# A long-convolution gate kernel on one core: the filter response made two pairs ahead, the first spectrum load cut in two, and the inverse result stored block by block

## The chip, the cores and the metric

The kernel runs on one core of one Trainium2 chip. The metric is the device time of one execution in microseconds (us). Three runs of the kernel before took 1207.08, 1214.94 and 1216.21 us (median 1214.94). The trace comes from one further, profiled execution.

The core has five engines with a queue of instructions each: PE (TensorE, matrix products into the PSUM memory), PEld (its weight loads), DVE (VectorE), ACT (ScalarE), POOL (GpSimd) and SP (SyncE, which here only issues DMAs). An engine takes its instructions in order; between engines there are semaphores. DMAs are issued from the queues of SP and ACT.

## The reference

```python
h    = (relu(pos_emb @ w1) @ w2) * exp(-0.01 * pos)      # the filter, S x D
u    = x * v
y    = irfft(rfft(u, 2S) * rfft(h, 2S))[:, :S]           # long convolution along the sequence
x2   = x * y
gate = sigmoid(causal_conv5(x2, conv_w))                 # per channel, 5 taps
out  = (gate * (x2 @ w_val)) @ w_out
```

B = 4, S = 12800, D = 128, 64 filter features, all float32.

## The kernel before

The transform of length 12800 is cut into J = 2 blocks of 6400 = N1 (100) x N2 (64), and both factors are done as matrix products. There are three stages.

**Stage 1** (0 to about 375 us) makes the first transform of u. It has 64 steps n, in 32 pairs q = n // 2 with s = n % 2. A step fetches 800 KB (`fetch`, split by `_Split`, L120, into 96 rows and 4 rows), multiplies x by v on DVE (`product`, L305), and each pair then takes sums and differences: two on DVE (L313) and two differences on POOL (L316). `spectra` (L321) does the matrix products into the PSUM tile `fp` and ACT copies them into `st` (L331, four buffers). `store` (L334) writes `st` to the DRAM tensor `a_u` one step later, as 96 and 4 rows. Between these steps the filter is made by the generator `filt` (L223): its steps are dealt out at a pace that has a number of the n steps as its divisor (L368, here N2 - 2), and its last part (tiles `fk` and `gp`, lines L274 to L288) uses ACT, DVE and PE.

**Stage 2** (about 375 to 804 us) runs over 50 pairs p of frequencies. `load_pair` (L427) brings 1 MB of `a_u` and, for every fourth pair, the tables `w`. `filter_pair` (F, L396) makes the filter's response: PE into a `c_ps` buffer, then three ACT operations into `h_sb` (L407 to L409, three buffers). `spectrum` (S0 and S1, L412) is the second transform: PE into four banks `z_ps`. `times` (L421) multiplies them on DVE: `va` and `vb` use the banks of S0, `vc` and `vd` those of S1. POOL adds (L514 to L516), and `inverse` (I0 and I1, L441) goes back: PE into `c_ps` (two buffers, shared with F), ACT into `c_sb` (L454), and a DMA to the DRAM tensor `c_y` (L457). The order is written out by hand. In one round the engines get: DVE va(p), vb(p), the small sums of p - 1 (L501 to L504), vc(p), vd(p); PE F(p+1), S0(p+1), S1(p+1), I0(p-1), I1(p-1); ACT the copies and DMA issues of I(p-1) and the three operations of F(p+1). DMAs from SP stand in program order.

**Stage 3** (815 us to the end) loads rows of `c_y` into the tile `ag` (`load_k`, L201, for the first three groups; these stand in SP's queue during stage 2 and at its end), sums over N1 on PE (`y_sum`, L597), transposes, multiplies by x and does the gate. `WARM` matrix products (L687), whose result nobody reads, stand on PE between the stages.

Lines used below: L120 the split DMA of stage 1 and 3; L436 the `a_u` loads; L431 the `w` loads; L417 S0 and S1; L402 F on PE; L447 the inverse on PE; L457 the `c_y` stores; L204 the early `ag` loads; L601 the first work of stage 3 on PE.

Of the kernel before, what the change touches and what calls it, by code (L numbers as in the profile page):

```python
# [24 lines left out]
J, N1, N2 = 2, 100, 64  # L25
M = N1 * N2
KG = 8
# [1 line left out]
P0 = NH - NF  # L29
PT = P0 + N1  # L30
R = 4
WARM = 8
NC1 = N1 // 2 + 1


# [88 lines left out]
def tile_longconv_gate(  # L124
# [20 lines left out]
    nc = tc.nc  # L145
# [5 lines left out]
    a_u = dram.tile([N1, 2, N2 // 2, 2, J, B, D], F32, name="a_u")  # L151

    c_y = dram.tile([J, N1, 2 * N2, B, D], F32, name="c_y")
# [30 lines left out]
    def load():  # L184
        return ld.tile([128, 2048], F32, name="ld")
# [10 lines left out]
    FIRST = len(blocks) // 2  # L196
# [4 lines left out]
    def load_k(s, c, k0, k1):  # L201
        j, g = y_order[s]
        n0 = c * N2 + g * R
        nc.sync.dma_start(  # L204
            out=block(s, c)[k0:k1], in_=c_y[j, k0:k1, n0:n0 + R].rearrange("k p b d -> k (p b d)"))


    with tc.tile_pool(name="p1", bufs=1) as p1, tc.tile_pool(name="ps1", bufs=1, space=PSUM) as ps1:
        pos_v = pos.rearrange("(j a n) f -> j a n f", j=J, a=N1)

# [97 lines left out]
        def mirrored(q):  # L308

            a, b = us.pop(2 * q), us.pop(2 * q + 1)  # L310
            eo = held_e[q % 2]
            for s, op in ((0, ALU.add), (1, ALU.subtract)):
                nc.vector.tensor_tensor(  # L313
                    eo[:PT, s].rearrange("p j l e -> p (j l e)"), a[:PT], b[:PT], op=op)
            for s in range(2):
                nc.gpsimd.tensor_tensor(  # L316
                    eo[:PT, s, :, 0], eo[:PT, s, :, 0], eo[:PT, s, :, 1], op=ALU.subtract)
            eos[q] = eo

# [14 lines left out]
        def store(q, s, st):  # L334
            sync_s.dma_start(
                out=a_u[:, s, q].rearrange("k e j b d -> k (e j b d)"),
                in_=st[P0:PT].rearrange("k e j b d -> k (e j b d)"))

        fetched, us, eos, last = {}, {}, {}, None
        with tc.manual_schedule():  # L340
            for t in held:
                nc.gpsimd.memset(t[0:P0], 0.0)
            held_e = [p1.tile([128, 2, J, 2, XE], F32, name=f"eo{i}") for i in range(2)]
            for t in held_e:
                nc.vector.memset(t[96:128], 0.0)
            fetch(0)
            raw_val, raw_out = _raw(nc, p1, w_val, "raw_val"), _raw(nc, p1, w_out, "raw_out")
            raw_cw = _raw(nc, p1, conv_w.rearrange("k d -> d k"), "raw_cw")
            fil = filt()
            n_fil, spent = 16 * 1.3 + 0.7 + 16 * 0.9 + 16 * 1.5 + 25 * 1.9 + 0.5, 0.0  # L350
            for i in range(1, XB):
                fetch(i)
            product(0)
            product(1)
            mirrored(0)
            product(2)
            for i in (XB, XB + 1):
                fetch(i)
            for n in range(N2):
                q, s = divmod(n, 2)  # L360
                if n + XB + 2 < N2:
                    fetch(n + XB + 2)
                if n + 3 < N2:
                    product(n + 3)
                if s == 0 and q + 1 < N2 // 2:
                    mirrored(q + 1)
                st = spectra(q, s)
                while spent < n_fil * (n + 1) / (N2 - 2):  # L368
                    step = next(fil, None)
                    if step is None:  # L370
                        break
                    spent += step
                if last:
                    store(*last)
                last = q, s, st
                if n == 40:
                    _narrow(nc, p1, wval, raw_val)
                if n == 46:
                    _narrow(nc, p1, wout, raw_out)
                if n == 52:  # L380
                    _narrow(nc, p1, cw, raw_cw)
            for _ in fil:
                pass
            store(*last)


    with tc.tile_pool(name="p2", bufs=1) as p2, tc.tile_pool(name="ps2", bufs=1, space=PSUM) as ps2:
        BD = B * D
        NP = N1 // 2
        PG = KG // 2  # L390
        half = [slice(h * N2, (h + 1) * N2) for h in range(2)]

        def bank():
# [18 lines left out]
        def spectrum(p, j):  # L412
            a2, wk = loaded[p]
            zs = bank(), bank()
            for c in range(2):
                for h in range(2):
                    nc.tensor.matmul(  # L417
                        out=zs[c][half[h]], lhsT=wk[half[c], 0, half[h]], rhs=a2[half[c], h, j], start=True, stop=True)
            z_p[p, j] = zs

        def times(out, z, h_sb, n):  # L421

            nc.vector.tensor_tensor(  # L423
                out, z.rearrange("p (b d) -> p b d", d=D).unsqueeze(1).to_broadcast([128, n, B, D]),
                h_sb.unsqueeze(2).to_broadcast([128, n, B, D]), op=ALU.mult)

        def load_pair(p):  # L427
            if p % PG == 0:
                n_p = min(PG, NP - p)
                wt = load().rearrange("p (k c e) -> p k c e", k=PG, c=4)[:, :, 0:3]  # L430
                nc.sync.dma_start(out=wt[:, 0:n_p], in_=t_w[:, p:p + n_p])  # L431
                weights.append(wt)
            a2 = load().rearrange("p (k j e) -> p k j e", k=2, j=J)
            step = 1 if p == 0 else 2
            for i in range(0, 2, step):
                nc.sync.dma_start(  # L436
                    out=a2[:, i:i + step].rearrange("p k j e -> p k (j e)"),
                    in_=a_u[2 * p + i:2 * p + i + step].rearrange("k s n e j b d -> (s n e) k (j b d)"))
            return a2, weights[-1][:, p % PG]

        def inverse(p, j, terms):  # L441
            wk = loaded[p][1]
            c_ps = ps2.tile([128, 2, BD], F32, name="c_ps", bufs=2)
            for i, (c, vt) in enumerate(terms):
                n = vt.shape[1] * D
                for h in range(2):
                    nc.tensor.matmul(  # L447
                        out=c_ps[:, h, 0:n], lhsT=wk[half[h], 1 + c], rhs=vt[half[h]].rearrange("p b d -> p (b d)"),
                        start=(i == 0), stop=(i == len(terms) - 1))
            if j == 0:  # L450
                c_sb = p2.tile([128, 2, J, B, D], F32, name="c_sb", bufs=2)
                outs[p] = c_sb
            c_sb = outs[p]
            nc.scalar.copy(out=c_sb[:, :, j].rearrange("p h b d -> p h (b d)"), in_=c_ps)  # L454
            if j == J - 1:
                for h in range(2):
                    nc.scalar.dma_start(  # L457
                        out=c_y[:, 2 * p + h].rearrange("j p b d -> p j (b d)"),
                        in_=c_sb[:, h].rearrange("p j b d -> p j (b d)"))

        weights, loaded, outs = [], {}, {}
        filt_p, z_p, v_p = {}, {}, {}
        AHEAD = 2
        PB = B // 2
# [1 line left out]
        def start_pair(p):  # L466
            filt_p[p] = filter_pair(p).rearrange("p s j c d -> p s (j c) d")
# [5 lines left out]
        with tc.manual_schedule():  # L473
            for p in range(-1, NP + 1):
                now, nxt, old = 0 <= p < NP, p + 1 < NP, 0 <= p - 1
                for q in range(AHEAD + 1) if p < 0 else (p + AHEAD,):
                    if q < NP and q not in loaded:
                        loaded[q] = load_pair(q)
                if p in early:
                    load_k(*early.pop(p))  # L480
                if p == 41:
                    j, g = y_order[0]
                    nc.sync.dma_start(
                        out=xr_first, in_=xt[j][:, g * R:(g + 1) * R].rearrange("d n b a -> d (n b a)"))
                if p == NP:
                    for s in range(FIRST):
                        for c in range(2):
                            load_k(s, c, 80, 96)
                if now:
                    h = filt_p.pop(p)  # L490
                    z0, z1 = z_p.pop((p, 0)), z_p.pop((p, 1))
                    va = p2.tile([128, 2 * J, B, D], F32, name="va", bufs=3)
                    vb = p2.tile([128, 2 * J, B, D], F32, name="vb", bufs=2)
                    times(va, z0[0], h[:, 0], 2 * J)
                    times(vb, z0[1], h[:, 1], 2 * J)
                if nxt:
                    start_pair(p + 1)
                    spectrum(p + 1, 0)
                if old:
                    oa, oc, od = v_p.pop(p - 1)  # L500
# [21 lines left out]
                    inverse(p - 1, 1, ((0, oa[:, 2]), (1, oa[:, 3, 0:PB]), (0, oc[:, 0]), (1, oc[:, 1])))  # L522
            for s in range(FIRST):
                for c in range(2):
                    load_k(s, c, 96, N1)

    ld_pool.__exit__(None, None, None)

# [6 lines left out]
    with tc.tile_pool(name="p3", bufs=1) as p3, tc.tile_pool(name="ps3", bufs=1, space=PSUM) as ps3:  # L535
# [144 lines left out]
        with tc.manual_schedule():  # L680
# [4 lines left out]
            for _ in range(WARM):  # L685
                w_ps = ps3.tile([D, 2 * D], F32, name="o_ps", bufs=2)
                nc.tensor.matmul(  # L687
                    out=w_ps, lhsT=ident, rhs=dft.rearrange("p a k -> p (a k)"), start=True, stop=True)
            for t in range(-AHEAD3, NT + 2):
                s = t + AHEAD3  # L690
# [79 lines left out]
```

## Time and profile before

| what | value |
|---|---|
| runs | 1207.08, 1214.94, 1216.21 us; median 1214.94 |
| profiled execution | 1216.66 us, its span 1214.6 us |
| mean granted TensorE clock | 0.971 |
| PE busy | 1069.3 us (88% of the span) |
| DVE busy | 979.5 us (81%) |
| POOL busy | 783.6 us (65%) |
| ACT busy | 615.1 us (51%) |
| DMA | 329.92 MB, mean 272 GB/s |

A row of a timeline reads: start in us, duration, engine, line, operation, the tile written and the tile read, shape, count, and in brackets how long the engine had been idle before it and what released it. "SPq" and "ACTq" are DMA issues. A row of windows gives, for a stretch of the span, the busy time of each engine, the granted TensorE clock (1.00 is full), the mean busy share of the sixteen DMA engines, and GB/s.

### The profile page before, as it was taken

Reading aid. Unit: us, or ns where it says so; the run is one execution under the profiler, and the core shown is the slowest. Engines: PE = TensorE matmul, PEld = TensorE weight load, DVE = VectorE, ACT = ScalarE, POOL = GpSimd, SP = SyncE. Lnnn points to the kernel's source line nnn. Section 1 sums busy time; section 2 is a strip of 40 time slices with the busy share of each in tenths; the row PEclk is TensorE's granted clock in tenths of the full one; section 3 lists DMA queues with packets and bytes.
Section 4 is the critical chain, followed back from the end, with each engine's and each line's share of the span. In section 5 each row is a group of like instructions: output and inputs, shape, how many; then the busy total and the mean of one; then the engine's idle time right before and its main releaser. Section 6 shows DMA issues by size and latency. Waiting matters only on the chain. (4 is left out here: it accounts for less than half of the span.)

```text
span 1214.6 us, 17869 instructions
## 1 busy us (share of the span) xinstructions
PE 1069.3 (88%) x6280; PEld 496.0 (41%) x6280; DVE 979.5 (81%) x1166; ACT 615.1 (51%) x1000; POOL 783.6 (65%) x400
## 2 busy tenths in 40 slices
PE   1689888777876999999999999978999999999986
PEld 0445455333442334443443444333444444444432
DVE  4477555588873899999999999926999999999997
ACT  0235654666672234333333433326676776766764
POOL 5134333233322788888888888826898898898880
PEclk9799999999897799999999999989999999999999
DMA  9899999999997578887777998767999989999932
GB/s 218 222 302 335 330 303 311 308 304 306 308 294 279 213 279 287 282 285 278 273 273 270 319 347 287 229 162 215 256 287 283 290 269 278 285 287 279 290 133 108
DMA packets 90976, 329.92 MB, mean 272 GB/s; under 512 B 10102, under 2 KB 17698, under 8 KB 77490
## 3 DMA queue, kind: packets, MB, share of 16 engines
q1 hardware_dynamic: 56912, 249.06, 67.5%
q10 hardware_dynamic: 33978, 79.74, 17.6%
q8 instruction: 51, 0.84, 0.3%
q14 instruction: 35, 0.29, 0.1%
HBM read 197.69 MB, written 131.07 MB: 271 GB/s over the span
## 5 line engine op out<-in xcount | busy, mean ns | idle before, releaser
L628 POOL TENSOR_TENSOR ext<-yr,xr 128x400 f32<-128x400 f32 x120 | 303.2, 2528 | 40.4 <-DVE yr L626 38.2
L316 POOL TENSOR_TENSOR eo<-eo 114x512 f32<-114x512 f32 x64 | 116.3, 1836 | 240.4 <-DVE eo L313 240.4
L329 PE MATMUL fp<-eo,fold 64*128 64x512 f32 x768 | 192.0, 633 | 63.1 <-ACT st L331 45.8
L643 DVE SCALAR_TENSOR_TENSOR gt<-ext,cw,gt 128x1600 f32<-128x1600 f32 x128 | 240.7, 1881 | 0.8 <-ACT gt L640 0.8
L454 ACT COPY c_sb<-c_ps 128x1024 f32<-128x1024 f32 x100 | 101.4, 1014 | 203.6 <-PE c_ps L447 194.2
L331 ACT COPY st<-fp 128x1024 f32<-128x1024 f32 x128 | 124.3, 1015 | 152.4 <-DMA a_u<-st 91.6
L447 PE MATMUL c_ps<-va,ld 64*128 64x512 f32 (+1 forms) x800 | 166.7, 556 | 0.7 <-POOL va L516 0.7
L423 DVE TENSOR_TENSOR va<-z_ps,h_sb 128x2048 f32<-128x2048 f32 x50 | 114.4, 2289 | 54.0 <-ACT h_sb L407 35.1
L417 PE MATMUL z_ps<-ld 64*64 64x512 f32 x800 | 142.3, 624 | 16.3 <-DMA ld<-a_u 7.3
L514 POOL TENSOR_TENSOR va<-va,vb 128x1024 f32<-128x1024 f32 x50 | 118.3, 2365 | 24.1 <-DVE vb L423 24.1
L601 PE MATMUL sd<-ag,inv 100*64 100x512 f32 x512 | 127.2, 612 | 7.3 <-DMA ag<-c_y 6.3
L329 PEld LDWEIGHTS fp<-eo,fold 64*128 64x128 f32 x768 | 73.6, 195 | 141.5 <-issue 81.3
L662 PE MATMUL o_ps<-gd,wout 128*128 128x400 f32 x256 | 112.4, 521 | 19.1 <-DVE gd L657 10.4
L447 PEld LDWEIGHTS c_ps<-va,ld 64*128 64x128 f32 x800 | 74.3, 189 | 114.1 <-issue 111.2
L516 POOL TENSOR_TENSOR va<-va,vb 128x1024 f32<-128x1024 f32 x50 | 118.5, 2370 | 0.0
L608 ACT COPY sd_sb<-sd 128x512 f32<-128x512 f32 x128 | 76.1, 594 | 81.2 <-PE sd L601 61.0
L423 DVE TENSOR_TENSOR vb<-z_ps,h_sb 128x2048 f32<-128x2048 f32 x50 | 114.0, 2280 | 0.0
L652 PE MATMUL v_ps<-ext,wval 128*128 128x400 f32 x256 | 107.1, 500 | 0.0
L447 PE MATMUL c_ps<-vc,ld 64*128 64x512 f32 x400 | 94.2, 589 | 0.0
L515 POOL TENSOR_TENSOR vc<-vc,vd 128x768 f32<-128x768 f32 x50 | 91.1, 1822 | 0.0
L615 PEld LDWEIGHTS tp<-ident,sd_sb 128*128 128x128 f32 x512 | 58.6, 141 | 75.9 <-PE sd L601 49.5
L615 PE MATMUL tp<-ident,sd_sb 128*128 128x128 f32 x512 | 80.3, 281 | 3.1 <-DVE yr L626 2.6
(88 smaller groups left out, 1493.3 us busy)
## 6 DMA issues: line engine op xcount, KB each, us to landing
c_y<-c_sb ACTq DMA_DIRECT2D x100, 512.0 KB
ld<-a_u SPq DMA_DIRECT2D x49, 1024.0 KB
ld<-in_xv_dram SPq DMA_DIRECT2D x64, 768.0 KB
a_u<-st SPq DMA_DIRECT2D x64, 768.0 KB
ag<-c_y SPq DMA_DIRECT2D x116, 384.0 KB
out_dram<-o_sb ACTq DMA_DIRECT2D x32, 800.0 KB
xr<-in_xt_dram SPq DMA_DIRECT2D x31, 800.0 KB
ld<-in_tab_w_dram SPq DMA_DIRECT2D x12, 768.0 KB
```

Source lines behind the costliest of these rows:

```text
L316: nc.gpsimd.tensor_tensor(eo[:PT, s, :, 0], eo[:PT, s, :, 0], eo[:PT, s, :, 1], op=ALU.subtract)
L329: nc.tensor.matmul(out=fp[:, h], lhsT=fold[r, w], rhs=eo[r, o, :, l], start=i == 0, stop=i == len(terms) - 1)
L331: nc.scalar.copy(out=st[:, o].rearrange("k j (h b) d -> k h j (b d)", h=2), in_=fp)
L417: nc.tensor.matmul(out=zs[c][half[h]], lhsT=wk[half[c], 0, half[h]], rhs=a2[half[c], h, j], start=True, stop=True)
L423: nc.vector.tensor_tensor(out, z.rearrange("p (b d) -> p b d", d=D).unsqueeze(1).to_broadcast([128, n, B, D]), h_sb.unsqueeze(2).to_broadc ...
L447: nc.tensor.matmul(out=c_ps[:, h, 0:n], lhsT=wk[half[h], 1 + c], rhs=vt[half[h]].rearrange("p b d -> p (b d)"), start=(i == 0), stop=(i == ...
L514: nc.gpsimd.tensor_tensor(va[:, 0:2], va[:, 0:2], vb[:, 0:2], op=ALU.add)
L516: nc.gpsimd.tensor_tensor(va[:, 2:4], va[:, 2:4], vb[:, 2:4], op=ALU.add)
L601: nc.tensor.matmul(out=sd[c * N2:(c + 1) * N2], lhsT=inv[:, c], rhs=ct[c][:, r * B * D:(r + 1) * B * D], start=True, stop=True)
L615: nc.tensor.transpose(out=tp[:, b], in_=t[:, b], identity=ident)
L628: nc.gpsimd.tensor_tensor(e[:, r0 + r], yr, xr, op=ALU.mult)
L643: nc.vector.scalar_tensor_tensor(gt, rows(t, k), cw[:, k:k + 1], gt, op0=ALU.mult, op1=ALU.add)
```

## The change

The edits, each with where it stands:

1. `WARM` from 8 to 14.
2. The filter's pace in stage 1: divisor N2 - 6 in place of N2 - 2, so that its steps are used up some four steps earlier.
3. The two differences of the last pair q = 31 are on DVE, each behind its sum or difference; those of all other pairs stay on POOL.
4. The first `a_u` load (p = 0) is cut. In place of two loads of 128 rows x 1024 behind the last store, the rows of the first 31 of 32 pairs q are loaded as two DMAs (62 rows x 2 x 1024, one for each s) ahead of the last store, and the rows of q = 31 as two DMAs of 2 rows x 2 x 1024.
5. S0 and S1 issue the products of c = 1 ahead of those of c = 0.
6. F runs two pairs ahead: round p makes F(p+2), and F(0), F(1) stand together at the start.
7. `c_y` is stored for each block j, right behind the copy of I0 or I1; before, both DMAs stood behind I1 and each held half of the rows for both j. Count (two a pair) and bytes are as before.
8. The last rows of `ag`: 4 rows by six loads at the end become 2 rows by six (rows 96 to 98), which need no pair later than p = 48, and behind them 2 rows by six (98 to 100), which need p = 49. All of these rows are of block j = 0.

```diff
-WARM = 8
+WARM = 14
...
+    def load_a(a2, p, n0, n1):
+        for s in range(2):
+            r = slice(s * N2 + 2 * n0, s * N2 + 2 * n1)
+            nc.sync.dma_start(
+                out=a2[r].rearrange("p k j e -> p k (j e)"),
+                in_=a_u[2 * p:2 * p + 2, s, n0:n1].rearrange("k n e j b d -> (n e) k (j b d)"))
...
+        if n1:
+            load_a(a2, p, 0, n1)
+        else:
+            nc.sync.dma_start(
+                out=a2.rearrange("p k j e -> p k (j e)"),
+                in_=a_u[2 * p:2 * p + 2].rearrange("k s n e j b d -> (s n e) k (j b d)"))
...
+            eng = nc.vector if q == N2 // 2 - 1 else nc.gpsimd
             for s, op in ((0, ALU.add), (1, ALU.subtract)):
                 nc.vector.tensor_tensor(
                     eo[:PT, s].rearrange("p j l e -> p (j l e)"), a[:PT], b[:PT], op=op)
-            for s in range(2):
-                nc.gpsimd.tensor_tensor(
+                eng.tensor_tensor(
                     eo[:PT, s, :, 0], eo[:PT, s, :, 0], eo[:PT, s, :, 1], op=ALU.subtract)
...
-                while spent < n_fil * (n + 1) / (N2 - 2):
+                while spent < n_fil * (n + 1) / (N2 - 6):
...
             for _ in fil:
                 pass
+            loaded[0] = load_pair(0, N2 // 2 - 1)
             store(*last)
...
-            for c in range(2):
+            for c in (1, 0):
...
-            if j == J - 1:
-                for h in range(2):
-                    nc.scalar.dma_start(
-                        out=c_y[:, 2 * p + h].rearrange("j p b d -> p j (b d)"),
-                        in_=c_sb[:, h].rearrange("p j b d -> p j (b d)"))
+            nc.scalar.dma_start(
+                out=c_y[j, 2 * p:2 * p + 2].rearrange("h p b d -> p h (b d)"),
+                in_=c_sb[:, :, j].rearrange("p h b d -> p h (b d)"))
...
+                if p < 0:
+                    load_a(loaded[0][0], 0, N2 // 2 - 1, N2 // 2)
...
+                    for s in range(FIRST):
+                        for c in range(2):
+                            load_k(s, c, 96, 98)
...
+                if p < 0:
+                    start_pair(0)
+                if p + 2 < NP:
+                    start_pair(p + 2)
                 if nxt:
-                    start_pair(p + 1)
                     spectrum(p + 1, 0)
...
-                    load_k(s, c, 96, N1)
+                    load_k(s, c, 98, N1)
```

Three places in the order of instructions are needed below. First, SP's queue at the end of stage 1, before; the 96- and 4-row DMAs are the stores of n = 62 and n = 63:

```order
L120 DMA a_u<-st 96x2048
L120 DMA a_u<-st 4x2048
L120 DMA a_u<-st 96x2048
L120 DMA a_u<-st 4x2048
L436 DMA ld<-a_u 128x1024 x2
L436 DMA ld<-a_u 128x2x1024 x3
```

The same place after the change; the first two rows are the store of n = 62, the sixth and seventh that of n = 63:

```order
L120 DMA a_u<-st 96x2048
L120 DMA a_u<-st 4x2048
L223 DMA ld<-in_tab_w_dram 128x4x384
L215 DMA ld<-a_u 62x2x1024 x2
L215 DMA ld<-a_u 2x2x1024
L120 DMA a_u<-st 96x2048
L120 DMA a_u<-st 4x2048
L215 DMA ld<-a_u 2x2x1024
L229 DMA ld<-a_u 128x2x1024 x3
```

The two 62-row loads and the first 2-row load now stand ahead of the store of n = 63, and so does the first load of `w`, which before stood in the middle of stage 1. The first 2-row load waits for the store of n = 62, the second for that of n = 63; three full loads follow.

Second, PE at the start of stage 2, before (L402 is F, L417 is S0 and S1, L447 the inverse):

```order
L402 MATMUL c_ps<-w2bd,ag 64x128 x8
L417 MATMUL z_ps<-ld 64x512 x8
L402 MATMUL c_ps<-w2bd,ag 64x128 x8
L417 MATMUL z_ps<-ld 64x512 x8
L402 MATMUL c_ps<-w2bd,ag 64x128 x8
L417 MATMUL z_ps<-ld 64x512 x8
L447 MATMUL c_ps<-va,ld 128x512 x6
```

After the change (L427 is F, L442 is S0 and S1, L458 the inverse):

```order
L427 MATMUL c_ps<-w2bd,ag 64x128 x16
L442 MATMUL z_ps<-ld 64x512 x8
L427 MATMUL c_ps<-w2bd,ag 64x128 x8
L442 MATMUL z_ps<-ld 64x512 x8
L427 MATMUL c_ps<-w2bd,ag 64x128 x8
L442 MATMUL z_ps<-ld 64x512 x8
L458 MATMUL c_ps<-va,ld 128x512 x6
```

F(0) and F(1) stand together at the start, and from there on F stands at the same place of each round as before, but is the one of the pair after next.

Third, ACT in one round of stage 2, before:

```order
L454 COPY c_sb<-c_ps 128x2x512 x2
L457 DMA c_y<-c_sb 128x2x512 x2
L407 COPY h_sb_2581<-c_ps 128x512
L408 ACTIVATE h_sb_2581<-c_ps 128x2x128
L409 COPY h_sb_2581<-c_ps 128x2x128
```

After:

```order
L465 COPY c_sb<-c_ps 128x2x512
L466 DMA c_y<-c_sb 128x2x512
L465 COPY c_sb<-c_ps 128x2x512
L466 DMA c_y<-c_sb 128x2x512
L432 COPY h_sb_2596<-c_ps 128x512
L433 ACTIVATE h_sb_2596<-c_ps 128x2x128
L434 COPY h_sb_2596<-c_ps 128x2x128
```

One of the two stores moved between the two copies; the three operations of F stay behind both.

More of the change, by code (lines that the diff above doesn't have):

```diff
@@ L205, in load_k, with load_pair @@
             out=block(s, c)[k0:k1], in_=c_y[j, k0:k1, n0:n0 + R].rearrange("k p b d -> k (p b d)"))
+    NP, PG = N1 // 2, KG // 2
+    weights, loaded = [], {}
+    def load_a(a2, p, n0, n1):
[4 more added lines that the diff above has]
+                in_=a_u[2 * p:2 * p + 2, s, n0:n1].rearrange("k n e j b d -> (n e) k (j b d)"))
+    def load_pair(p, n1=None):
+        if p % PG == 0:
+            n_p = min(PG, NP - p)
+            wt = load().rearrange("p (k c e) -> p k c e", k=PG, c=4)[:, :, 0:3]
+            nc.sync.dma_start(out=wt[:, 0:n_p], in_=t_w[:, p:p + n_p])
+            weights.append(wt)
+        a2 = load().rearrange("p (k j e) -> p k j e", k=2, j=J)
+        if n1:
[4 more added lines that the diff above has]
+                in_=a_u[2 * p:2 * p + 2].rearrange("k s n e j b d -> (s n e) k (j b d)"))
+        return a2, weights[-1][:, p % PG]
     with tc.tile_pool(name="p1", bufs=1) as p1, tc.tile_pool(name="ps1", bufs=1, space=PSUM) as ps1:
@@ L388, in tile_longconv_gate @@
         BD = B * D
-        NP = N1 // 2
-        PG = KG // 2
         half = [slice(h * N2, (h + 1) * N2) for h in range(2)]
@@ L425, in times @@
                 h_sb.unsqueeze(2).to_broadcast([128, n, B, D]), op=ALU.mult)
[L427 to L439, printed above, removed]
         def inverse(p, j, terms):
@@ L454, in inverse @@
             nc.scalar.copy(out=c_sb[:, :, j].rearrange("p h b d -> p h (b d)"), in_=c_ps)
-            if j == J - 1:
-                for h in range(2):
-                    nc.scalar.dma_start(
-                        out=c_y[:, 2 * p + h].rearrange("j p b d -> p j (b d)"),
-                        in_=c_sb[:, h].rearrange("p j b d -> p j (b d)"))
-        weights, loaded, outs = [], {}, {}
+            nc.scalar.dma_start(
+                out=c_y[j, 2 * p:2 * p + 2].rearrange("h p b d -> p h (b d)"),
+                in_=c_sb[:, :, j].rearrange("p h b d -> p h (b d)"))
+        outs = {}
         filt_p, z_p, v_p = {}, {}, {}
```

## The prediction

> **What bounds the kernel now.** I read the page first, its parts 2 and 5.
>
> ```profile
> span 1214.6 us, 17869 instructions
> PEclk9799999999897799999999999989999999999999
> DMA  9899999999997578887777998767999989999932
> L423 DVE TENSOR_TENSOR va<-z_ps,h_sb 128x2048 f32<-128x2048 f32 x50 | 114.4, 2289 | 54.0 <-ACT h_sb L407 35.1
> ```
>
> A slice is 30.4 us. The DMA row is full in stage 1 (slices 1 to 12), falls at the change to stage 2 (slices 13, 14), is at 7 to 8 tenths in most of stage 2 and dips again at the change to stage 3 (slice 26). So the two changes of stage, and a loop that the DMA row doesn't fill, are where the edits can act. The last row says that DVE stood idle 35.1 us ahead of `va`, until ACT had made the filter's response `h_sb`. Where that wait comes from is in the timeline of two rounds of stage 2:
>
> ```profile
> 444.94 2.29 DVE L423 TENSOR_TENSOR va<-z_ps,h_sb 128x2048 f32<-128x2048 f32 x1 [1.32 <-ACT h_sb L407]
> ...
> 452.40 2.28 DVE L423 TENSOR_TENSOR va<-z_ps,h_sb 128x2048 f32<-128x2048 f32 x1
> ...
> 452.53 0.19 PEld L417 LDWEIGHTS z_ps<-ld 64*64 64x64 f32 x4 [0.94 <-DVE vd L423]
> ...
> 453.54 3.28 PE L447 MATMUL c_ps<-va,ld 64*128 64x512 f32 x16
> ...
> 458.46 0.67 PE L402 MATMUL c_ps<-w2bd,ag 64*64 64x128 f32 x16
> 458.58 1.01 ACT L454 COPY c_sb<-c_ps 128x1024 f32<-128x1024 f32 x1 [1.99 <-PE c_ps L447]
> 458.72 1.21 DVE L423 TENSOR_TENSOR vd<-z_ps,h_sb 128x1024 f32<-128x1024 f32 x1
> ...
> 458.95 2.11 PE L417 MATMUL z_ps<-ld 64*64 64x512 f32 x16
> ...
> 459.62 0.89 ACTq L457 DMA_DIRECT2D c_y<-c_sb  x2
> ...
> 460.61 0.59 ACT L407 COPY h_sb<-c_ps 128x512 f32<-128x512 f32 x1 [1.02 <-PE z_ps L417]
> ...
> 461.23 2.29 DVE L423 TENSOR_TENSOR va<-z_ps,h_sb 128x2048 f32<-128x2048 f32 x1 [1.30 <-ACT h_sb L407]
> ```
>
> The starts of `va` show a short pair (452.40 - 444.94 = 7.46 us) and a long one (461.23 - 452.40 = 8.83). In the short one DVE never stops. In the long one a ring closes: PE waits for DVE's `vd` to free a bank (452.53), runs S1 and the inverse (453.54 to 458.46, 4.92 us), then F; ACT copies `c_sb` (458.58), issues two DMAs (459.62, 0.89 us) and only then makes `h_sb` (460.61), and `va` starts at 461.23. The new S0 is there earlier: its half of the 2.11 us from 458.95 ends near 460.00. How often this occurs is in the rows of the whole loop:
>
> ```profile
> 412.33 2.29 DVE L423 TENSOR_TENSOR va<-z_ps,h_sb 128x2048 f32<-128x2048 f32 x1 [5.00 <-ACT h_sb L407]
> ...
> 788.32 2.29 DVE L423 TENSOR_TENSOR va<-z_ps,h_sb 128x2048 f32<-128x2048 f32 x1 [1.21 <-ACT h_sb L407]
> ...
> L423 DVE TENSOR_TENSOR va<-z_ps,h_sb 128x2048 f32<-128x2048 f32 x46 | 105.3, 2289 | 34.0 <-ACT h_sb L407 33.9
> ...
> 412.30:788.30 376.00, 368.70 (x2578) 152.23 (x2576) 345.77 (x322) 145.56 (x231) 310.55 (x183) 1.00 0.82 284
> 700.00:720.00 20.00, 19.72 (x134) 8.37 (x130) 18.73 (x20) 7.34 (x11) 16.66 (x11) 1.00 1.04 393
> ```
>
> From `va`(3) at 412.33 to `va`(49) at 788.32 lie 46 pairs, 8.17 us each. PE is busy 368.70 of 376.00 us there, but partly with matmuls drawn out by waits for banks; DVE's idle is the 34.0 us ahead of `va`.
>
> **Part by part. F two pairs ahead.** It adds nothing; F(p+2) stands where F(p+1) stood. `va`(p+1) then needs S0(p+1) and a response a whole pair old. In the long pair it starts near 460.05 (S0's end plus 0.05; DVE itself is free at 458.72 + 1.21 = 459.93), in place of 461.23: 1.18 us sooner. What is late next is the same ring without ACT in it: `vd`, S1, inverse, F, S0, `va`. Two pairs go from 7.46 + 8.83 = 16.29 to 15.11 us, and 23 such doubles give **27.1 us**. The upper bound is all of DVE's idle, 34.0 us; the lower bound is 0, if another wait takes its place. The `va`(3) wait (5.00 us, part of a start at a low clock) I cost at 1.2 with the same reasoning, between 0 and 5.0. `c_y` by block puts one DMA issue (half of 0.89 us) between the copies of I0 and I1; ACT is busy 145.56 of 376 us, so its idle time hides that; uncovered it is 0.45 us a pair, 22 us in all, and after F has moved nobody waits for it in the same pair. The order of c puts the bank that `va` reads second; since 460.00 is the end of both, it is in the sum already, and at most half of S0's 1.05 us, 0.5 a long pair, could have been had without it (12 us in all).
>
> **The change to stage 2.** The rows of before:
>
> ```profile
> 362.75 3.45 POOL L316 TENSOR_TENSOR eo<-eo 114x512 f32<-114x512 f32 x2 [6.38 <-DVE eo L313]
> ...
> 363.73 3.15 DVE L277 SCALAR_TENSOR_TENSOR fk<-dft,tw,fk 128x128 f32<-128x128 f32 x4
> ...
> 367.35 2.85 PE L329 MATMUL fp<-eo,fold 64*128 64x512 f32 x12
> ...
> 369.43 1.93 ACT L331 COPY st<-fp 128x1024 f32<-128x1024 f32 x2 [1.39 <-PE fp L329]
> ...
> 374.48 0.68 SPq L120 DMA_DIRECT2D a_u<-st  x2
> ...
> 379.01 2.37 SPq L436 DMA_DIRECT2D ld<-a_u  x5
> ...
> 382.45 4.01 PE L417 MATMUL z_ps<-ld 64*64 64x512 f32 x13 [7.27 <-DMA ld<-a_u]
> ...
> 385.68 2.29 DVE L423 TENSOR_TENSOR va<-z_ps,h_sb 128x2048 f32<-128x2048 f32 x1 [18.80 <-PE z_ps L417]
> ...
> 381.00:383.00 2.00, 0.55 (x1) 0.28 (x2) 0.00 (x0) 0.00 (x0) 0.00 (x0) 0.50 1.01 399
> 812.00:813.00 1.00, 0.00 (x0) 0.00 (x0) 0.00 (x0) 0.00 (x0) 0.00 (x0) 1.00 0.22 66
> 811.50:814.70 3.20, 0.00 (x0) 0.02 (x1) 0.00 (x0) 0.00 (x0) 0.00 (x0) 0.84 0.31 48
> ```
>
> Before, the last store is issued at 374.48, is there at 379.01 (4.5 us), and the load takes 3.4 us more (382.45). The store of n = 62 could go at 371.4 (369.43 + 1.93). After the pace change the filter's steps (363.73) are gone from here, and the last differences, which POOL ended at 362.75 + 3.45 = 366.20, are on DVE, where `fk` ran: half of the 1.21 us that a twice as large `vd` takes, 0.6 each (bounds 0.5, and POOL's 1.7). So the matmuls of 367.35 can start some 2.7 us sooner; without both edits POOL alone would allow 1.1. And 768 KB of `w`, at 399 GB/s 1.9 us, leave a stage that the DMA row fills. I take the store of n = 62 at T = 366 (365 to 369).
>
> Then the new loads. Of 62-row loads the trace has no row. Loads of 128 rows keep all sixteen engines busy (share 1.01, 399 GB/s, 381 to 383). Loads of 4 rows, alone in flight at 811.5 to 814.7, reach a share of 0.31 and 48 GB/s, or 0.22 and 66 GB/s in the one clean microsecond: four or five engines of sixteen. The number of rows therefore sets how many engines work. The two 62-row loads hold 62 x 2 x 4 KB x 2 = 1.016 MB: **2.5 us** at 399 GB/s, **15.4** at 66, **21.2** at 48. All rows that fill the engines have counts that sixteen divides (16, 64, 96, 128); 62 and 4 are not of these. So I take the 4-row end, 21.2 us, and keep 2.5 for the range.
>
> The Trainium skill, page "DMA: Bandwidth & Descriptors", section "Why a DMA increments its semaphore by 16 and not by 1", says that a DMA is spread over the largest number of engines up to 16 that divides its slowest dimension on both sides, and on this kind of queue over the lowest-numbered ones. By that rule 4 rows use 4 engines, which the share of 0.22 to 0.31 agrees with, and 62 rows use 2; an estimate by it is 1.016 MB at 2/16 of 399 GB/s, 20.4 us. No row here shows a 62-row load.
>
> The path: T = 366; ahead of the loads 800 KB of store and 768 KB of `w` at 399 GB/s, 4.0; the loads 21.2; the share of the last store that queues behind them on the same engines (800 KB at 399 GB/s), 2.0; the last 2-row load, which waits for that store, 3.4 from issue to use as before. S0(0) at 396.6 in place of 382.45: **14.2 us later**. By the 66 GB/s row it is 8.4 later. With all sixteen engines the end is set by the last store (T + 3 for `st`) behind 3.4 MB of traffic (8.5 us) and the 2-row load: near 379, 3.4 sooner.
>
> **The change to stage 3.**
>
> ```profile
> 799.95 1.01 ACT L454 COPY c_sb<-c_ps 128x1024 f32<-128x1024 f32 x1 [1.00 <-PE c_ps L447]
> ...
> 804.71 1.83 ACTq L457 DMA_DIRECT2D c_y<-c_sb  x2
> ...
> 804.74 3.72 PE L687 MATMUL o_ps<-dft,ident 128*128 128x256 f32 x16 [1.11 <-ACT c_sb L454]
> ...
> 814.71 4.93 PE L601 MATMUL sd<-ag,inv 100*64 100x512 f32 x8 [6.25 <-DMA ag<-c_y]
> ...
> 820.59 1.94 PE L601 MATMUL sd<-ag,inv 100*64 100x512 f32 x8
> ...
> SPq L204 <- DMA c_y<-c_sb: 9.2, 1, 9.2
> ```
>
> SP waits 9.2 us for the last `c_y` store before it issues the last `ag` loads; the store was issued at 804.71, and PE starts stage 3 at 814.71, 10.0 us later. All the rows wanted are of j = 0, and after the change their store goes out behind the copy of 799.95, near 801.0. Then the data are there near 811.0. Fourteen warm products take 3.72 x 14/8 = 6.5 us and end at 811.25, so PE starts at about 811.25: 3.5 us sooner, with no idle time ahead of it (after the idle time before 382.45 the clock was 0.50, row 381 to 383). The six further load issues are SP's, which waits there anyway. The first eight `sd` took 4.93 us there and 1.94 a moment later: 3.0 more. Together **6.5 us**; bounds 3.0 (only the clock) and 8.0.
>
> **Sum**, against the profiled execution's 1216.66: + 14.2 - 1.2 - 27.1 - 6.5 = 1196.1. That execution lies 1.7 above the median of 1214.94, so I say **1194**. What a measurement of this kernel can tell from no change is about 1%, 12 us.
>
> **Rivals.** *A. The 62-row loads are spread like 128-row ones.* Then 1216.66 - 3.4 - 34.8 = 1178.5. For it: the 399 GB/s row, and 62 is near 64. Against: the share of 0.22 to 0.31. Chance 0.15.
> *B. The loop meets another wait and gives half.* 284 GB/s over 8.17 us is 2.32 MB a pair, which at 7.555 us is 307 GB/s. For it: from 700 to 720, where early `ag` loads come on top, the engines are full (1.04 at 393 GB/s) and a shorter round asks for still more there. Against: the loop as a whole has a share of 0.82. Half of 27.1 lost: 1196.1 + 13.5 = 1209.6, within 1%. Chance 0.13.
> *C. Slower: the 62-row loads crawl on one engine.* If a 4-row load's 48 GB/s is that of four engines, one moves 12 GB/s and 1.016 MB takes 85 us, 64 more than forecast: 1260. It decides from 33 us more than forecast (1229, slower by 1%), which is 54 us for the loads or 19 GB/s. Against: the share falls with the rows of a load, and 62 are more than 4. Chance 0.05.
> That F ahead doesn't remove the wait at all is the far end of B: 1223, within 1%; its chance, 0.02, is in "same".
>
> **How the numbers follow.** Forecast 0.65 with its own range of 1187 to 1206 (66 GB/s to a start 3 us worse, loop 24 to 30), A 0.15, B 0.13, far B 0.02, C 0.05. To hold 8 in 10 the range takes in A, to 1177, and most of B, to 1210. Faster by over 1% (under 1203): most of the forecast (0.61) and A (0.15), 0.76. Within 1%: 0.04 + 0.13 + 0.02, 0.19. Slower 0.05.
>
> **What the changed profile would show.** Right: two 62-row loads near 368, a DMA share near 2/16 to 5/16 for 15 to 21 us, S0(0) at 391 to 398; `va` starts alternating 7.5 and 7.6 us, DVE's idle ahead of `va` under 10 us, its releaser PE `z_ps`; the first `sd` near 811 less the shift, taking under 2.5 us. Wrong: S0(0) before 385 (A), `va` waiting for `z_ps` or `ld` by over 0.6 us a pair (B), S0(0) behind 430 (C).

## The result and the profile after

The changed kernel took 1195.84 us (median of 4 runs, 1193.04 to 1196.86) beside 1215.55 for the kernel before on the same chip: 0.985 of its time, 95% interval 0.9803 to 0.9897. Forecast were 1194 us and a range of 1177 to 1210. The profiled execution took 1193.04 us, with a span of 1191.2 in place of 1214.6. One execution of an experiment below (a_cut24) took 3598.16 us where its other three took 1178 to 1182; it is left out of that kernel's median, and no trace shows why it was long.

The page of the changed kernel, the lines that answer to those of before:

```profile
span 1191.2 us, 17916 instructions
...
PEclk9798999999996599999999999999999999999999
DMA  9899999999994678888888998686999899999932
...
L448 DVE TENSOR_TENSOR va<-z_ps,h_sb 128x2048 f32<-128x2048 f32 x50 | 114.3, 2286 | 52.6 <-PE z_ps L442 52.6
```

Three things moved. The low place at the change to stage 2 got deeper: the clock is at 6 and 5 tenths in slices 13 and 14, and the DMA row at 4 and 6. The DMA row in most of stage 2 rose from 7 and 8 to 8. And `va` waits no longer for `h_sb`: its 52.6 us stand to S0's account, 45.3 of them ahead of the first `va` alone. The loop by itself, first the timeline's rows of `va`(3) and `va`(49), then DVE's group of the 46 `va` from the one up to the other (busy us, mean ns, idle before):

```profile
419.82 2.29 DVE L448 TENSOR_TENSOR va<-z_ps,h_sb 128x2048 f32<-128x2048 f32 x1 [2.64 <-PE z_ps L442]
...
769.28 2.28 DVE L448 TENSOR_TENSOR va<-z_ps,h_sb 128x2048 f32<-128x2048 f32 x1
```

```profile
L448 DVE TENSOR_TENSOR va<-z_ps,h_sb 128x2048 f32<-128x2048 f32 x46 | 105.2, 2286 | 7.2 <-PE z_ps L442 7.2
```

46 pairs take 349.46 us (7.60 each) in place of 375.99, and DVE's idle time there fell from 34.0 to 7.2 us. The timeline of two rounds shows the ring without ACT:

```profile
450.23 2.29 DVE L448 TENSOR_TENSOR va<-z_ps,h_sb 128x2048 f32<-128x2048 f32 x1 [0.21 <-PE z_ps L442]
...
457.17 0.37 ACTq L466 DMA_DIRECT2D c_y<-c_sb  x1
457.63 0.59 ACT L432 COPY h_sb<-c_ps 128x512 f32<-128x512 f32 x1 [0.49 <-PE z_ps L442]
457.70 2.28 DVE L448 TENSOR_TENSOR va<-z_ps,h_sb 128x2048 f32<-128x2048 f32 x1
...
463.76 0.67 PE L427 MATMUL c_ps<-w2bd,ag 64*64 64x128 f32 x16
...
464.25 2.11 PE L442 MATMUL z_ps<-ld 64*64 64x512 f32 x16
...
465.44 2.29 DVE L448 TENSOR_TENSOR va<-z_ps,h_sb 128x2048 f32<-128x2048 f32 x1 [0.21 <-PE z_ps L442]
```

The pairs now alternate between 7.47 and 7.74 us. At 457.63 ACT only begins the response, and `va` at 457.70 doesn't care: it uses the one made a round ago.

The change from stage 1 to stage 2 in the timeline (the row of 367.65 is the third of the loads grouped at 361.70), and behind it two windows (busy time of each engine, clock, DMA share, GB/s):

```profile
358.05 1.36 SPq L120 DMA_DIRECT2D a_u<-st  x2
...
360.12 1.01 ACT L357 COPY st<-fp 128x1024 f32<-128x1024 f32 x1 [0.72 <-PE fp L355]
...
361.70 13.79 SPq L215 DMA_DIRECT2D ld<-a_u  x3
...
367.65 7.84 SPq L215 DMA_DIRECT2D ld<-a_u  x1
375.54 1.37 SPq L120 DMA_DIRECT2D a_u<-st  x2
391.51 0.24 SPq L215 DMA_DIRECT2D ld<-a_u  x1
...
393.36 3.79 PE L442 MATMUL z_ps<-ld 64*64 64x512 f32 x16 [31.07 <-DMA ld<-a_u]
...
395.54 2.29 DVE L448 TENSOR_TENSOR va<-z_ps,h_sb 128x2048 f32<-128x2048 f32 x1 [45.34 <-PE z_ps L442]
```

```profile
365.00:375.00 10.00, 0.00 (x0) 0.00 (x0) 0.00 (x0) 0.00 (x0) 0.00 (x0) 0.50 0.13 53
376.00:386.00 10.00, 0.00 (x0) 0.00 (x0) 0.00 (x0) 0.00 (x0) 0.00 (x0) 0.50 0.35 123
```

The last `st` is ready at 361.13, but S0(0) starts at 393.36. For ten microseconds the DMA share is 0.13, which is the time of two engines of sixteen, at 53 GB/s. The third load's issue alone holds SP for 7.84 us (the one at 391.51 takes 0.24), so the last store, ready for 14 us, goes out at 375.54, and the load that waits for it is issued at 391.51.

The change from stage 2 to stage 3:

```profile
781.90 1.01 ACT L465 COPY c_sb<-c_ps 128x1024 f32<-128x1024 f32 x1 [0.70 <-PE c_ps L458]
...
785.74 0.37 ACTq L466 DMA_DIRECT2D c_y<-c_sb  x1
786.15 1.01 ACT L465 COPY c_sb<-c_ps 128x1024 f32<-128x1024 f32 x1 [3.23 <-DMA c_y<-c_sb]
787.21 6.31 PE L704 MATMUL o_ps<-dft,ident 128*128 128x256 f32 x28 [2.35 <-ACT c_sb L465]
...
793.51 2.69 PE L618 MATMUL sd<-ag,inv 100*64 100x512 f32 x8
```

The copy of block 0 ends at 782.91, but its store goes out only at 785.74. The chain of work that ended last, in order of time, shows what ACT waited for, an older `c_y` store that took 7.44 us to land:

```profile
778.23 7.44 DMA c_y<-c_sb
...
785.74 0.37 ACTq L466
```

The copy of block 1 stands behind that store on ACT, and the warm products behind that copy; they then run straight into stage 3.

### The profile page after: what moved, and what is told of

Its sections match the earlier page's. It is cut to its first block, busy times and chain, and to the rows that moved or that the text cites. A ratio compares the mean times of both kernels' runs of the same rounds, so it can differ in the third digit from the quotient of the medians.

```text
span 1191.2 us, 17916 instructions
## 1 busy us (share of the span) xinstructions
PE 1047.2 (88%) x6292; PEld 497.7 (42%) x6292; DVE 981.2 (82%) x1168; ACT 616.6 (52%) x1000; POOL 781.2 (66%) x398
## 4 chain that ended last, share of the span: by engine, by line
PE 61%; DMA 27%; DVE 5%; ACT 4%; issue 2%; SPq 1%; POOL 0%; ACTq 0%; DVEq 0%
DMA a_u<-st 20%; PE c_ps L458 20%; PE z_ps L442 9%; PE sd L618 9%; PE o_ps L679 6%; PE v_ps L669 5%; PE tp L632 4%; PE fp L355 4%; PE c_ps L427 2%; DMA ag<-c_y 2%; DVE gt L660 2%; DMA ld<-in_pos_emb_dram 1%; PE gp L269 1%; DMA w1bd<-in_w_dram 1%; DMA tw<-in_tab_tw_dram 1%
## 5 line engine op out<-in xcount | busy, mean ns | idle before, releaser
L342 POOL TENSOR_TENSOR eo<-eo 114x512 f32<-114x512 f32 x62 | 112.5, 1832 | 223.1 <-DVE eo L340 223.1
L458 PE MATMUL c_ps<-va,ld 64*128 64x512 f32 (+1 forms) x800 | 165.2, 552 | 0.0
L448 DVE TENSOR_TENSOR va<-z_ps,h_sb 128x2048 f32<-128x2048 f32 x50 | 114.3, 2286 | 52.6 <-PE z_ps L442 52.6
L442 PE MATMUL z_ps<-ld 64*64 64x512 f32 x800 | 122.6, 620 | 32.5 <-DMA ld<-a_u 31.1
L458 PEld LDWEIGHTS c_ps<-va,ld 64*128 64x128 f32 x800 | 74.0, 188 | 112.2 <-issue 111.2
L458 PE MATMUL c_ps<-vc,ld 64*128 64x512 f32 x400 | 94.2, 589 | 0.0
L340 DVE TENSOR_TENSOR eo<-u,ld 114x1024 f32<-114x1024 f32 x64 | 78.8, 1266 | 10.0 <-PE fp L355 6.6
```

What stands on the lines that cost most here:

```text
L442: nc.tensor.matmul(out=zs[c][half[h]], lhsT=wk[half[c], 0, half[h]], rhs=a2[half[c], h, j], start=True, stop=True)
L448: nc.vector.tensor_tensor(out, z.rearrange("p (b d) -> p b d", d=D).unsqueeze(1).to_broadcast([128, n, B, D]), h_sb.unsqueeze(2).to_broadc ...
L458: nc.tensor.matmul(out=c_ps[:, h, 0:n], lhsT=wk[half[h], 1 + c], rhs=vt[half[h]].rearrange("p b d -> p (b d)"), start=(i == 0), stop=(i == ...
```

## The experiments

Each comparison has its own runs of the kernel before; the medians of those were 1214.34 us (for a_cut30 to a_noF), 1214.58 (b_cy to a_no4_c01) and 1213.62 (the last three). The table has starts in the profiled execution of each kernel, in us: the end of the last copy into `st`, S0(0), `va`(3), `va`(49), the first row of POOL's `tail` in stage 3, and the span; the last column is the median of the runs.

| kernel | last st | S0(0) | va(3) | va(49) | tail | span | median |
|---|---|---|---|---|---|---|---|
| before | 374.45 | 382.45 | 412.33 | 788.32 | 821.92 | 1214.6 | 1215.55 |
| changed | 361.13 | 393.36 | 419.82 | 769.28 | 798.04 | 1191.2 | 1195.84 |
| a_cut30 | 362.12 | 378.20 | 405.85 | 755.33 | 784.89 | 1177.6 | 1179.53 |
| a_cut24 | 362.88 | 377.72 | 404.52 | 754.02 | 785.66 | 1178.6 | 1180.38 |
| a_no4 | 366.03 | 376.14 | 404.29 | 753.78 | 783.12 | 1176.8 | 1179.80 |
| a_noF | 365.18 | 395.82 | 422.90 | 785.66 | 813.33 | 1206.4 | 1208.69 |
| b_cy | 369.74 | 377.62 | 406.82 | 769.63 | 797.14 | 1191.1 | 1192.56 |
| b_F | 375.74 | 383.77 | 411.63 | 763.86 | 797.79 | 1190.5 | 1190.94 |
| b_s1 | 368.76 | 379.06 | 408.54 | 784.36 | 818.49 | 1212.8 | 1211.19 |
| a_no4_c01 | 369.57 | 379.03 | 406.74 | 755.54 | 783.67 | 1177.1 | 1179.05 |
| a_w8 | 367.68 | 377.97 | 405.52 | 754.96 | 783.53 | 1176.8 | 1179.18 |
| a_wtail | 365.89 | 378.67 | 407.24 | 756.67 | 786.29 | 1179.1 | 1178.03 |
| a_best | 365.29 | 377.94 | 405.70 | 755.40 | 784.94 | 1178.0 | 1177.43 |

**The rows of the first load.** Two kernels move the cut from 31 to 30 and to 24:

```diff
-            loaded[0] = load_pair(0, N2 // 2 - 1)
+            loaded[0] = load_pair(0, 30)
...
-                    load_a(loaded[0][0], 0, N2 // 2 - 1, N2 // 2)
+                    load_a(loaded[0][0], 0, 30, N2 // 2)
```

> The changed kernel with the first a_u load cut at 30 pairs of rows in place of 31: two loads of 60 rows and two of 4 in place of 62 and 2; everything else as changed. Theory D (a load runs on as many engines as the largest divisor of its rows up to 16): 60 rows run on 15 engines, the two loads take some 3 us in place of 26, the last store is issued and lands sooner, S0(0) starts near 371 to 375 in place of 393.4, and the time is 1173 to 1178. Rival R (the engines used grow smoothly with the rows, or a load in two strided parts is slow as such): 60 rows go like 62, S0(0) near 393, time 1193 to 1198.

> The changed kernel with the first a_u load cut at 24: two loads of 48 rows and two of 16, both on all sixteen engines by theory D. Theory D: S0(0) near 370 to 374, time 1172 to 1177, within 2 us of the cut at 30. Rival R: fewer rows are slower or the same, S0(0) at 393 or later. Rival P (what costs is that the loads stand ahead of the last store on SP, and not their rows): S0(0) near 390, time 1192 to 1196.

Measured: 0.9707 of the time before for both (0.9664 to 0.975 and 0.9664 to 0.9751), some 16 us less than the changed kernel. Two rows fewer in each of two loads did this. The timeline and a window of the cut at 30, and a window of the cut at 24:

```profile
362.98 2.33 SPq L215 DMA_DIRECT2D ld<-a_u  x3
365.40 0.99 SPq L120 DMA_DIRECT2D a_u<-st  x2
375.71 0.25 SPq L215 DMA_DIRECT2D ld<-a_u  x1
...
378.20 3.64 PE L442 MATMUL z_ps<-ld 64*64 64x512 f32 x16 [14.92 <-DMA ld<-a_u]
```

```profile
366.00:370.00 4.00, 0.00 (x0) 0.00 (x0) 0.00 (x0) 0.00 (x0) 0.00 (x0) 0.50 1.02 254
...
366.00:370.00 4.00, 0.00 (x0) 0.00 (x0) 0.00 (x0) 0.00 (x0) 0.00 (x0) 0.50 1.05 191
```

Three loads are issued within 2.33 us, the last store at once behind them, and the engines are full (1.02, and 1.05 with 48 rows). So rival R (few rows, few engines, smoothly) and rival P (the place on SP) fall. By the rule of the Trainium skill quoted with the prediction (page "DMA: Bandwidth & Descriptors", section "Why a DMA increments its semaphore by 16 and not by 1"), 62 rows go to 2 engines, 60 to 15 and 48 to 16. The share of 0.13 and the jump between 62 and 60 agree with it; 15 can't be told from 16 in these windows, in which other traffic runs too. S0(0) came 3 to 4 us later than theory D said, and the times 1.5 and 3.4 us above its ranges: the last store needed 10 us from issue to landing behind `w` and the loads.

**Without the cut.**

```diff
-            nc.sync.dma_start(
-                out=a2.rearrange("p k j e -> p k (j e)"),
-                in_=a_u[2 * p:2 * p + 2].rearrange("k s n e j b d -> (s n e) k (j b d)"))
+            step = 1 if p == 0 else 2
+            for i in range(0, 2, step):
+                nc.sync.dma_start(
+                    out=a2[:, i:i + step].rearrange("p k j e -> p k (j e)"),
+                    in_=a_u[2 * p + i:2 * p + i + step].rearrange("k s n e j b d -> (s n e) k (j b d)"))
...
-            loaded[0] = load_pair(0, N2 // 2 - 1)
...
-                if p < 0:
-                    load_a(loaded[0][0], 0, N2 // 2 - 1, N2 // 2)
```

> The changed kernel without the cut of the first a_u load: two loads of 128 rows behind the last store, w back in the middle of stage 1. Theory: the store of n = 62 goes out near 360, the last store lands near 367, the load takes 3.4 us, S0(0) near 370 to 373 in place of 393.4, time 1173 to 1178: the cut costs some 20 us where it stands. Rival: the early start of stage 1's end comes from w's move or from the loads themselves, S0(0) near 382 as before the change, time 1184 to 1188.

Measured: 0.9706 (0.9668 to 0.9744), S0(0) at 376.14, later than the 370 to 373 expected. The two plain loads do as well as the cuts at 30 and 24. With these the last copy was ready some 3 to 7 us sooner (`w` is out of stage 1; but a_wtail and a_best, without the cut and with `w` out, had 365 to 366, so the gain can't be put down to `w`), but then S0 needs 15 to 16 us more in place of 9 to 10. The cut is thus worth nothing here, and with 62 rows it costs about 16 us.

**F ahead and the stores by block, each alone and each left out.** a_noF makes F(p+1) again in the changed kernel; b_F and b_cy put one edit each into the kernel before:

```diff
 # b_F
+                if p < 0:
+                    start_pair(0)
+                if p + 2 < NP:
+                    start_pair(p + 2)
                 if nxt:
-                    start_pair(p + 1)
 # b_cy
-            if j == J - 1:
-                for h in range(2):
-                    nc.scalar.dma_start(
...
+            nc.scalar.dma_start(
+                out=c_y[j, 2 * p:2 * p + 2].rearrange("h p b d -> p h (b d)"),
+                in_=c_sb[:, :, j].rearrange("p h b d -> p h (b d)"))
```

> The changed kernel with F one pair ahead as before, all else as changed. Theory: DVE waits for h_sb again in every second pair, 46 pairs at 8.17 us in place of 7.60, time 1195.8 + 26.5 = 1222 (1218 to 1226). Rival: the store between the two copies had already let ACT reach h_sb sooner (one DMA issue of 0.45 us less behind the second copy), so that a part of the gain stays: 0.45 us in 23 rounds, 10 us, time near 1212.

> The kernel before with one edit: F two pairs ahead (edit 6). Theory: va no longer waits for h_sb wherever the stores stand, so the double pair takes 15.1 to 15.2 us, 23 x 1.1 = 25 us, time 1188 to 1191 beside 1215. Rival (the gains of the two edits add up): F ahead alone gives 13 to 14 us, time near 1201.

> The kernel before with one edit: c_y stored by block, each right behind its copy (edit 7). Theory: one DMA issue of some 0.45 us less stands between the second copy and h_sb in the long pair, so the double pair goes from 16.29 to 15.77 us as in the changed kernel without F ahead: 23 x 0.52 = 12 us, time 1202 to 1205 beside 1215; DVE's wait for h_sb in the loop falls from 33.9 to about 21 us. Rival (the store's place only matters at the end of stage 2): 1 to 3 us.

Measured: a_noF 0.9946 (0.9918 to 0.9974), b_F 0.9808 (0.9746 to 0.9869), b_cy 0.9822 (0.9756 to 0.9888). The group of `va` over the loop, in a_noF, b_cy and b_F:

```profile
L448 DVE TENSOR_TENSOR va<-z_ps,h_sb 128x2048 f32<-128x2048 f32 x46 | 105.3, 2289 | 20.1 <-ACT h_sb L432 20.1
```

```profile
L423 DVE TENSOR_TENSOR va<-z_ps,h_sb 128x2048 f32<-128x2048 f32 x46 | 105.2, 2288 | 21.2 <-ACT h_sb L407 21.2
```

```profile
L423 DVE TENSOR_TENSOR va<-z_ps,h_sb 128x2048 f32<-128x2048 f32 x46 | 105.2, 2288 | 10.1 <-PE z_ps L417 10.1
```

The loop (`va`(49) less `va`(3) in the table) takes 376.0 us before, 362.8 with the stores by block alone, 352.2 with F ahead alone and 349.5 with both. So they don't add: both shorten the same wait for `h_sb`. Stores by block take one DMA issue out from between the second copy and `h_sb` (13 of the 34 us of the wait); F ahead takes `h_sb` out of the ring (24 us, all of it but 10.1). For a_noF the rival was right, with 12.9 us lost and not 26. For b_F the theory held: 1190.94 us, where 1188 to 1191 was expected. For b_cy the loop gave 13.2 us, as its theory said (12); what both stories left out is 6.1 us at the change to stage 3 (`tail` less `va`(49): 27.5 in place of 33.6). A further 5.5 us (`va`(3) at 406.82 in place of 412.33) came ahead of the loop, where the two kernels are alike, so that part is not the edit's.

**The tail of stage 1** (edits 2 and 3 in the kernel before):

```diff
-                while spent < n_fil * (n + 1) / (N2 - 2):
+                while spent < n_fil * (n + 1) / (N2 - 6):
...
+            eng = nc.vector if q == N2 // 2 - 1 else nc.gpsimd
...
-            for s in range(2):
-                nc.gpsimd.tensor_tensor(
+                eng.tensor_tensor(
```

> The kernel before with edits 2 and 3 alone (the filter's pace and the last pair's differences on DVE). Theory: the last stage 1 store goes out some 6 us sooner than at 374.48, S0(0) near 376 in place of 382.45, time 1208 to 1210 beside 1215. Rival: stage 1 is bound by its loads and the tail moves by 2 us at most, 1213.

Measured: 0.9978 (0.9948 to 1.0009), 3.4 us between the medians, not clear of no change. The last copy came at 368.76; three kernels with stage 1 as before had 374.45, 369.74 and 375.74, so one profile can't size it better than to some 5 us.

**The order of c, the warm products and the place of w**, each on top of a_no4, and the three together:

```diff
 # a_no4_c01
-            for c in (1, 0):
+            for c in (0, 1):
 # a_w8
-WARM = 14
+WARM = 8
 # a_wtail: the first w load, ahead of the last store
-        if p % PG == 0:
+        if p % PG == 0 and p // PG == len(weights):
...
+            wt = load().rearrange("p (k c e) -> p k c e", k=PG, c=4)[:, :, 0:3]
+            nc.sync.dma_start(out=wt, in_=t_w[:, 0:PG])
+            weights.append(wt)
             store(*last)
```

> The changed kernel without the cut of the first load and with c = 0 issued first, as before. Theory: PE's first half of S1 no longer waits for vd, the ring gets shorter and DVE's wait of 0.21 us in every second pair goes: up to 23 x 0.2 = 5 us, time 1175 beside 1180. Rival: both halves run beside each other and end together in both orders, no change, 1178 to 1181.

> The changed kernel without the cut of the first load (time 1179.8) and with 8 warm products in place of 14. Theory: with the store of block j = 0 out sooner the wait behind 8 products is about 2 us, as in the kernel before with stores by block alone (2.37 us, first sd at nearly full clock), so the six further products buy nothing and, where they run at half clock (8.0 us), hold sd back: time 1178 to 1180, from va(49) to the first tail row 27.5 to 28.5 us in place of 29.3. Rival (the forecast's): without them sd falls to half clock, 3 us slower, 1183.

> The changed kernel without the cut of the first load, but with the first load of w left where the change has it, just ahead of the last store. Theory: w's 768 KB in the middle of stage 1 cost some 5 us there (last copy into st ends near 363 in place of 368) and in the tail 2 us at most, so S0(0) comes near 373 in place of 377.6: time 1175 to 1177 beside 1179.8. Rival: the last store queues behind w and gives all of it back, S0(0) near 377, no change.

> The last two together and c = 0 first: no cut of the first load, w just ahead of the last store, 8 warm products, the rest as changed. Theory: the gains of the two add up, 1174 to 1177, at any rate under the changed kernel's 1195.8 by 15 to 22 us. Rival: neither does anything, 1179.

Measured: 0.9708 (0.9639 to 0.9778), 0.9709 (0.9681 to 0.9738), 0.9702 (0.9672 to 0.9731) and, all three, 0.9683 (0.9653 to 0.9713), beside 0.9706 without them: none is clear of no change by itself. The order of c moved the wait ahead of every second `va` from 0.21 to 0.16 us, and the loop from 349.5 to 348.8, where up to 5 us was expected. `w` in the tail got the last copy done at 365 to 366, but S0(0) came at 378 as before: the rival was right. With 14 warm products a_no4 spent 8.00 us on them; with 8, PE stood idle for 1.07 us ahead of `sd`:

```profile
772.74 5.32 PE L703 MATMUL o_ps<-dft,ident 128*128 128x256 f32 x16 [2.20 <-ACT c_sb L466]
779.12 2.56 PE L617 MATMUL sd<-ag,inv 100*64 100x512 f32 x8 [1.07 <-DMA ag<-c_y]
```

These rows are of a_w8. Its low clock lay in the warm products (0.50 from 772.70 to 776.00, so that 16 rows took 5.32 us) and not in `sd`, where it was 1.00. From `va`(49) to `tail` it took 28.6 us, a_no4 29.3. The lowest median is that of a_best, 1177.43 us, 18 us under the changed kernel and 36 under the one before; it is not clear of the other three or of a_no4.

## Why the prediction was right, point by point

The time was 1.8 us off. The terms were off by up to 4 us, on both sides, so that the small error of the whole is partly luck.

- **F two pairs ahead.** Forecast 27.1 us from 46 pairs, measured 375.99 - 349.46 = 26.5, with the mechanism said: the ring `vd`, S1, inverse, F, S0 is what is left (7.47 and 7.74 us; 15.21 for two, forecast 15.11). The stores by block were counted at nothing, and beside F ahead they are nearly that (2.7 us in the loop, the order of c included). But the reason that ACT's idle time hides the DMA issue holds only there: alone, the same edit is worth 13.2.
- **`va`(3).** Forecast 1.2; from `va`(0) to `va`(3) it was 24.28 in place of 26.65 us, 2.4.
- **The start.** Forecast S0(0) 14.2 us later, measured 10.9 (9.9 at `va`(0)). Two errors partly cancelled. T, the store of n = 62, was said 366 and was 358: the tail of stage 1 ended 13.3 us sooner, where a kernel with edits 2 and 3 alone gained 5.7 and the kernels that also have `w` out of stage 1 ended between 361 and 366. And from T to S0(0) it took 35.3 us in place of 30.6. The term that was too small is the loads with the last store's share behind them: forecast 21.2 + 2.0, measured 29.8 from the first issue (361.70) to the last store's landing (391.51).

```profile
380.00:382.00 2.00, 0.00 (x0) 0.00 (x0) 0.00 (x0) 0.00 (x0) 0.00 (x0) 0.50 0.14 59
382.00:387.00 5.00, 0.00 (x0) 0.00 (x0) 0.00 (x0) 0.00 (x0) 0.00 (x0) 0.50 0.13 52
388.00:391.00 3.00, 0.00 (x0) 0.00 (x0) 0.00 (x0) 0.00 (x0) 0.00 (x0) 0.50 0.06 26
```

By 380 the share is back at two engines (0.14), so most of the last store had been moved, and two engines, at the end one (0.06), worked on until it landed. That SP was held until 375.54 is thus not shown to have cost anything here; why the two needed 6.6 us more than forecast stays open. What holds an issue for 7.84 us the rows don't say either; the queue of the two busy engines is the likely place, and no run here tested it.

The rate in this term was luck in part. The forecast took 48 GB/s from a stretch of before in which it had 4-row loads alone in flight; but nothing moved until 812, and two 800 KB loads were issued at 813.58:

```profile
811.50:812.00 0.50, 0.00 (x0) 0.00 (x0) 0.00 (x0) 0.00 (x0) 0.00 (x0) 1.00 0.00 0
...
813.58 0.84 SPq L550 DMA_DIRECT2D xr<-in_xt_dram  x2
```

That stretch had a share of 0.31, the 62-row loads 0.13: the 53 GB/s came near 48 with fewer engines. And the argument that only counts divisible by sixteen fill the engines falls with the 60 rows of a_cut30.

- **The change to stage 3.** Forecast 6.5, measured 33.60 - 28.76 = 4.8 (`va`(49) to `tail`). The first `sd` came 24.23 us behind `va`(49) in place of 26.39, 2.2 sooner where 3.5 was forecast; from it to `tail` it took 4.53 in place of 7.21 us, 2.7 less where 3.0 was forecast. The step that failed is that the store of block 0 goes out right behind its copy, near 801.0 by the times of before, 12.7 us behind `va`(49). It went out 16.46 behind it, no sooner than the two stores of before (16.39), because ACT held it for the older store; block 1's copy was held with it, and the warm products ended 24.2 us behind `va`(49), 1.3 later than forecast. In b_cy the store wasn't held. It went out 12.81 us behind `va`(49) and `sd` started 22.50 behind it, near the forecast's 22.9:

```profile
781.40 1.01 ACT L454 COPY c_sb<-c_ps 128x1024 f32<-128x1024 f32 x1 [0.70 <-PE c_ps L447]
782.44 0.37 ACTq L455 DMA_DIRECT2D c_y<-c_sb  x1
...
792.13 1.04 PE L599 MATMUL sd<-ag,inv 100*64 100x512 f32 x2 [2.37 <-DMA ag<-c_y]
```

The changed kernel and the eight made from it hold the store by 1.7 to 3.6 us. F ahead, the cut, the order of c and the number of warm products are each undone in one of them, so the hold needs none of these; between edits 2, 3 and 8 as its cause no run decides.

The six further warm products show no gain: stores by block with 8 of them took 27.5, 28.6 and 29.5 us (b_cy, a_w8, a_best), with 14 seven kernels took 27.7 to 31.6. The 14 held PE for 6.31 to 9.28 us, against 6.5 said. In the changed kernel the granted clock was 1.00 in them; in a_no4 (8.00 us) and a_cut24 (9.28) it was low at first:

```profile
771.40:775.00 3.60, 3.59 (x9) 2.91 (x10) 0.00 (x0) 0.00 (x0) 0.00 (x0) 0.55 0.65 243
...
772.60:776.00 3.40, 3.33 (x8) 2.70 (x9) 0.00 (x0) 0.02 (x1) 0.00 (x0) 0.50 0.69 263
```

The length of the idle time ahead of them doesn't decide it alone: it was 2.35 us in the changed kernel and 2.04 in a_no4. The page "TensorE: Matmul & The Clock Gate" of the Trainium skill (section "What's actually happening") says that the window in which the chip watches PE's activity runs freely, so that the count of slow matmuls varies from run to run. The 6.31, 8.00 and 9.28 us that the same 28 rows took in different kernels agree.

- **Stage 3 itself** took 393.2 in place of 392.7 us behind `tail`.

9.9 - 2.4 - 26.5 - 4.8 + 0.5 = -23.3, and the spans differ by 23.4. Of the signs that the prediction named, two missed by little: the 62-row loads stood at 361.70 and not near 368, and the first `sd` took 2.69 us and not under 2.5, at a clock of 1.00.

Rival A priced a first load that runs on all engines: it said S0(0) near 379 (its own figures, 366 or 369 with 8.5 and 3.4, give 377.9 or 380.9) and 1178.5 us, and the kernels with 60 and 48 rows had S0(0) at 378 and took 1179.5 and 1180.4. Rivals B and C did not occur: the DMA share of the loop rose from 0.82 to 0.87 without new waits for loads, the rate from 284 to 305 GB/s, about the 307 at which B saw the danger:

```profile
419.80:769.30 349.50, 349.50 (x2564) 153.71 (x2556) 344.88 (x323) 145.53 (x230) 312.30 (x183) 1.00 0.87 305
```

## What to carry to other kernels

Look at the number of rows of every DMA that is cut: 62 rows kept two engines of sixteen busy (share 0.13) where 60 and 48 filled them (1.02 and 1.05), and behind the slow loads the next issue was held too. Before two edits on one ring are credited with a gain each, do each alone: here 13 and 24 us made 26.5 together. A load put early only pays if what it waits for last isn't queued behind it. And see whether a store that is issued sooner also leaves sooner: here an older one held it.

## What the runs showed that I had not expected

- Two DMAs on two engines (share 0.13, 53 GB/s) held back what followed on the same queue: the issue of a small load behind them took 7.84 us, and the last store was there 16 us after its issue at 375.54, in place of 4.5.
- A store issued from ACT waited there for an older store to land (785.74, 2.8 us), and the copy behind it was held with it (ACT stood idle for 3.23 us).
- The time that stage 1 takes differs by some 6 us between kernels in which it is the same (last copy at 369.74 to 375.74).
